# First batch of a pooled-attention and MLP kernel: a broadcast, a bias row and the rests of k placed elsewhere, and the first MLP products in smaller pieces

## The chip, the cores and the metric

The kernel runs on one core of a Trainium2 chip. The metric is device time in microseconds (us) for one execution; the figure given for a kernel is the median of its runs. The core has a matrix engine (TensorE, in the profile PE, with its weight loads as PEld), VectorE (DVE), ScalarE (ACT), GpSimd (POOL) and SyncE (SP), which mostly issues DMA transfers. Each engine works through its own instructions in the order in which the program lists them; between engines semaphores hold the order of data.

## The reference

Eight batches, eight heads, 576 tokens, 64 columns a head; everything in float32.

```python
# attention with k and v averaged over groups of 8 tokens (576 -> 72)
k_p = k.reshape(B, H, 72, 8, D).mean(axis=3)
v_p = v.reshape(B, H, 72, 8, D).mean(axis=3)
scores = matmul(q, k_p.transpose(0, 1, 3, 2)) / sqrt(D)
scores = scores - max(scores, axis=-1, keepdims=True)
attn = exp(scores); attn = attn / (sum(attn, axis=-1, keepdims=True) + 1e-09)
x = matmul(attn, v_p)                      # then laid out as batch x 576 x 512
# mixing over tokens, then an MLP over channels
a1 = alpha1 * x + beta1
tok = einsum('ts,bsd->btd', w_tok, a1)     # w_tok 576 x 576
u = x + lam * tok
a2 = alpha2 * u + beta2
out = u + lam * (maximum(a2 @ w_ch1, 0.0) @ w_ch2)   # 512 -> 2048 -> 512
```

## The kernel before, in words

The 576 tokens of a batch are handled as 512 in four chunks of 128, and a rest of 64; the rests of two batches make one more chunk. So eight batches give 36 chunks, and four chunks make one of nine blocks of 512 tokens for the MLP. While block n goes through the MLP, the attention of batch n+1 is woven into it by a list of pieces with due times (`todo`, L712 to L747). Batch 0 has no MLP to be woven into: its pieces stand one after the other in lines L583 to L662, and this written order is the order of every engine's queue. The change touches only these lines.

The pieces that matter here:

- `keep_warm(n)` (L64): n matmuls of 128x512 on constants, whose result nobody reads.
- `broadcast(i)` (L264): a float32 matmul of a column of ones with one row of `vecs`, which puts that row on all 128 partitions. Row 0 is lam, row 1 lam times alpha1 (multiplied at L262 on DVE). ACT copies the results to `lam_bc` (L586) and `lamal_bc` (L588). `lamal_bc` is first read by `att_X`.
- `cast_q` (L128) and `cast_rem` (L117) turn q and the rests of q and k into bf16; `cast_rem` also sums the rests of k (L123, L124). `sum_k` (L133: L138, L139) and `sum_v` (L412: L416, L418) add the tokens of a group. Ahead of `sum_v(0, 1)` on POOL a memset of one column of the other v tile (L613) makes POOL wait until DVE is done with it.
- `row_of_xs` (L270, instruction L273): the product of beta1 and lam, as an additional row of `xs`, through which beta1 enters the token mixing.
- `att_F` (L362) transposes q for four heads on PE, ACT copies (L373); `att_Frem` (L377) does it for the rests; `att_K` (L393) pools k with matmuls (L401 and, for the rests, L404), copied at L408. `att_S` (L446) makes the scores of one head (L453) and their exponentials on ACT (L455). `att_V`, `att_Vrem` (L421, L437) do for v what `att_K` does for k (matmuls L424, L442; copies L428, L444). `att_AV` (L459) multiplies weights and v (L470, L473) and divides by the row sums on DVE (L475, L477). `att_X` (L480) multiplies x by `lamal_bc` into `xs` (L484, L488).
- `setup_wtok` (L281) transposes a strip of w_tok (PE L288, ACT copy L291), `setup_rowsum` (L294) makes row sums of it (L300, copy L302), `setup_vectors` (L276) turns beta2 (L278, L279), `setup_bias` (L346) makes the MLP's bias from it (L351, L353).
- `mix_T` (L504): five matmuls (L512), the sum u on DVE (L514), and the product with alpha2 (L516). `mix_uT` (L519): four transposes (L527) and an ACT copy into `u_fm` (L529), which holds a block of 512 tokens.
- `mlp_A(n, j, t0, t1)` (L537): four matmuls (L543) for 128 of the 2048 hidden columns and tokens t0 to t1 of the block; the ReLU on ACT (L548) follows when all 512 tokens are there. `mlp_B` (L553, matmuls L566) is the second product.

Loads are issued by SP in the order of the program, except the weights, which POOL issues (`load_wtok` L147, `load_w1` L324, `load_w2` L329). Batch 1's loads (`load_qk(1, 0)` and the following, L631 to L636) stand behind a DVE memset (L82) that comes after `att_AV(0, 5)`. All PSUM results of these pieces but the broadcasts' come from a pool of six buffers (`gp`), the broadcasts' from a pool of two that the MLP's second product uses later.

Of the kernel before, what the change touches and what calls it, by code (L numbers as in the profile page):

```python
# [23 lines left out]
def kernel(  # L24
# [18 lines left out]
    nc = tc.nc  # L43
# [20 lines left out]
    def keep_warm(count):  # L64

        ps = gp("ps_warm")
        for _ in range(count):
            nc.tensor.matmul(out=ps, lhsT=warm[:, 0:P], rhs=warm)
# [48 lines left out]
    def cast_rem(b, eng, copy=None):  # L117
        raw = st1[b]["rem_raw"]
        rq = work.tile([P, 4, D], BF, tag="rem_q", bufs=2, name="rem_q")
        rk = work.tile([P, 2, D], BF, tag="rem_k", bufs=2, name="rem_k")  # L120
        (copy or eng.tensor_copy)(out=rq, in_=raw[:, 0])
        t = raw[:, 1]
        eng.tensor_tensor(out=t[:, 0:2], in0=t[:, 0:2], in1=t[:, 2:4], op=ALU.add)  # L123
        eng.tensor_tensor(out=rk, in0=t[:, 0:1].to_broadcast((P, 2, D)),  # L124
                          in1=t[:, 1:2].to_broadcast((P, 2, D)), op=ALU.add)
        st1[b]["rem"] = rq, rk
# [137 lines left out]
    def broadcast(i):  # L264

        ps = psB.tile([P, DM], FP, tag="ch", bufs=2, name="ps_bc")
        nc.tensor.matmul(out=ps, lhsT=ones_row, rhs=vecs[0:1, i])
        return ps

    def row_of_xs(i, eng):  # L270

        p0 = 64 - 64 * i
        eng.tensor_tensor(out=xs_pool[i][p0:p0 + 1, 4, :], in0=vecs[p0:p0 + 1, 2],  # L273
                          in1=vecs[p0:p0 + 1, 0], op=ALU.mult)

    def setup_vectors():  # L276
        ps = gp("ps_vec")
        nc.tensor.transpose(out=ps[:, 0:4], in_=b2row, identity=identity[0:4, 0:4])  # L278
        nc.scalar.copy(out=b2c_bf, in_=ps[:, 0:4])  # L279

    def setup_wtok(tcx, copy):  # L281

        trc = P if tcx < 4 else REM
        w = wt_bf[0:trc, S * tcx:S * tcx + 640]
        strided = w[:, 0:512].rearrange("p (m c) -> p c m", c=4)
        ps_w = gp("ps_w").bitcast(BF)
        for sc in range(5):
            nc.tensor.transpose(out=ps_w[0:P, trc * sc:trc * sc + trc],  # L288
                                in_=strided[:, sc, :] if sc < 4 else w[:, 512:640],
                                identity=identity_bf[0:trc, 0:trc])  # L290
        copy(out=wtT[:, 0:5, P * tcx:P * tcx + trc],  # L291
             in_=ps_w[:, 0:5 * trc].rearrange("p (s t) -> p s t", t=trc))

    def setup_rowsum(tcx):  # L294

        trc = P if tcx < 4 else REM
        cols = slice(P * tcx, P * tcx + trc)
        ps = gp("ps_rs")
        for sc in range(5):
            nc.tensor.matmul(out=ps[:, 0:trc], lhsT=ones_bf if sc < 4 else ones_lo,  # L300
                             rhs=wtT[:, sc, cols], start=(sc == 0), stop=(sc == 4))
        nc.scalar.copy(out=wtT[64:65, 4, cols], in_=ps[64:65, 0:trc])  # L302
# [43 lines left out]
    def setup_bias(g):  # L346
        ps_bias = gp("ps_bias")
        for i in range(4):
            jc = 4 * g + i
            for cc in range(4):  # L350
                nc.tensor.matmul(out=ps_bias[0:P, i:i + 1], lhsT=w1_of(cc, jc),  # L351
                                 rhs=b2c_bf[:, cc:cc + 1], start=(cc == 0), stop=(cc == 3))
        nc.scalar.copy(out=bias_cols[:, 4 * g:4 * g + 4], in_=ps_bias[0:P, 0:4])  # L353
# [39 lines left out]
    def att_K(b, u, *copies):  # L393

        st = st1[b]
        ps_kp = gp("ps_kp")


        kp = ps_kp[:, 0:320].rearrange("p (r h y) -> p r h y", r=2, h=2)
        for e in range(2):  # L400
            nc.tensor.matmul(out=kp[:, :, :, 8 + 32 * e:40 + 32 * e],  # L401
                             lhsT=st["k"][u][:, e].rearrange("p t d -> p (t d)"), rhs=sel_k)
        kp = ps_kp[:, 0:320].rearrange("p (r y) -> p r y", r=2)
        nc.tensor.matmul(out=kp[:, :, 72:88], lhsT=st["rem"][1].rearrange("p t d -> p (t d)"),  # L404
                         rhs=pool_rem[:, 4 * u:4 * u + 4])
        for j in range(2):
            rows = slice(64 * j, 64 * j + 64)
            copies[j % len(copies)](  # L408
                out=kpT_pool[u][rows, j].rearrange("p r (h x) -> p r h x", h=2)[:, :, :, 0:72],
                in_=kp[rows, :, 8:152].rearrange("p r (h x) -> p r h x", h=2))  # L410
# [26 lines left out]
    def att_Vrem(b, copy):  # L437

        ps_v = gp("ps_v")
        vr = ps_v[:, 0:264].rearrange("p (a x) -> p a x", x=66)  # L440
        for a in range(4):
            nc.tensor.matmul(out=vr[:, a], lhsT=sel_rem[:, a], rhs=vrem_pool[b % 2])  # L442
        for hh, rows in ((0, slice(64, 72)), (1, slice(32, 64))):
            copy(out=vp1_pool[b % 2][hh][rows], in_=vr[rows])  # L444

    def att_S(b, h):  # L446

        st = st1[b]
        u, r, hh = h // 4, h // 2 % 2, h % 2
        ET, n = ET_pool[(8 * b + h) % 6], P if hh else SPG  # L450
        for j in range(2):
            ps_sc = gp("ps_sc")
            nc.tensor.matmul(out=ps_sc[0:n, 0:288], lhsT=kpT_pool[u][:, j, r, 72 * hh:72 * hh + n],  # L453
                             rhs=st["qT"][u][:, h % 4, :])
            nc.scalar.activation(out=ET[0:n, 64 + j:64 + S + j:2], in_=ps_sc[0:n, 0:288],  # L455
                                 func=AF.Exp, bias=0.0, scale=1.0 / 64)
        st["ET"][h] = ET

    def att_AV(b, h):  # L459
        st = st1[b]  # L460
        if "x" not in st:
            st["x"] = work.tile([P, 5, DM], FP, tag="x_tm", bufs=1, name="x_tm")
        hp, hh = h // 2, h % 2
        n = P if hh else SPG
        ET, vp1, x = st["ET"][h][0:n], vp1_pool[b % 2][hh][0:n, hp], st["x"]
        ps_av = gp("ps_av")
        av = ps_av[:, 0:5 * 66].rearrange("p (c x) -> p c x", x=66)
        for c in range(4):
            m0 = 64 + 256 * (c // 2) + c % 2
            nc.tensor.matmul(out=av[:, c, :], lhsT=ET[:, m0:m0 + 256:2], rhs=vp1)  # L470

        r0 = 576 - 64 * (b % 2)
        nc.tensor.matmul(out=av[:, 4, :], lhsT=ET[:, r0:r0 + 128], rhs=vp1)  # L473
        rec = work.tile([P, 5], FP, tag="rec", bufs=2, name="rec")
        nc.vector.reciprocal(out=rec, in_=av[:, :, 64:65])  # L475
        dd = D * h
        nc.vector.tensor_tensor(out=x[:, :, dd:dd + D], in0=av[:, :, 0:64],  # L477
                                in1=rec.unsqueeze(2).to_broadcast((P, 5, D)), op=ALU.mult)

    def att_X(b, h0, h1, eng=nc.vector):  # L480

        x, xs = st1[b]["x"], xs_pool[b % 2]
        cols = slice(D * h0, D * h1)
        eng.tensor_tensor(  # L484
            out=xs[:, 0:4, cols], in0=x[:, 0:4, cols],
            in1=lamal_bc[:, cols].unsqueeze(1).to_broadcast((P, 4, D * (h1 - h0))), op=ALU.mult)
        p0 = 64 * (b % 2)
        eng.tensor_tensor(out=xs[p0:p0 + 64, 4, cols], in0=x[p0:p0 + 64, 4, cols],  # L488
                          in1=lamal_bc[p0:p0 + 64, cols], op=ALU.mult)
# [91 lines left out]


    new_batch(1)  # L583
    keep_warm(4)
    ps_lam = broadcast(0)
    nc.scalar.copy(out=lam_bc, in_=ps_lam)  # L586
    ps_lamal = broadcast(1)
    nc.scalar.copy(out=lamal_bc, in_=ps_lamal)  # L588
    cast_q(0, 0, nc.vector.tensor_copy)
    att_F(0, 0)  # L590
    fill_E()
    sum_k(0, 0, nc.vector)
    cast_rem(0, nc.gpsimd)
    cast_q(0, 1, nc.gpsimd.tensor_copy)
    row_of_xs(0, nc.vector)
    att_Frem(0, (0,), nc.scalar.copy)
    att_K(0, 0, nc.vector.tensor_copy, nc.scalar.copy)
    att_Frem(0, (1,), nc.vector.tensor_copy)
# [7 lines left out]
    att_F(0, 1)  # L606
    att_S(0, 2)
    att_K(0, 1, nc.vector.tensor_copy)
    att_S(0, 3)
    v_00 = st1[0]["v"][0]  # L610
    sum_v(0, 0)
    att_Vrem(0, nc.scalar.copy)
    nc.gpsimd.memset(v_00[:, 0, 0, 0:1], 0.0)  # L613
    sum_v(0, 1, nc.gpsimd)
    att_S(0, 4)
# [19 lines left out]
    load_v(1, 0)  # L635
    load_v(1, 1)  # L636
    att_X(0, 4, 6, nc.gpsimd)
    setup_wtok(2, nc.scalar.copy)
    att_AV(0, 6)
    setup_rowsum(0)  # L640
    setup_rowsum(1)
    setup_wtok(3, nc.scalar.copy)
    att_AV(0, 7)
    att_X(0, 6, 8)
    setup_rowsum(2)
    setup_rowsum(3)
    setup_vectors()
    keep_warm(2)
    mix_T(0, 0)
    mix_T(0, 1)  # L650
    mix_T(0, 2, nc.gpsimd)
    mix_uT((0, 0))
    mix_T(0, 3)
    mix_uT((0, 1))
    setup_bias(0)
    for j in range(4):
        mlp_A(0, j, 0, 256)
        if j in (1, 2):
            mix_uT((0, 1 + j))
    for j in range(4):  # L660
        mlp_A(0, j, 256, 512)
    fill_v(1)  # L662
# [115 lines left out]
```

The softmax here doesn't subtract the row's maximum and nothing guards it: scores larger than these inputs give would overflow.

## Time and profile before

| | |
|---|---|
| median of 5 runs | 369.96 us (369.43 to 370.4) |
| profiled execution | 370.38 us, of which span 368.6 us |
| mean granted clock of PE | 0.995 |
| busy, share of the span: PE, DVE, ACT, POOL | 97%, 60%, 58%, 34% |
| chain that ended last | PE 86%, DMA 4%, POOL 4%, ACT 3% |
| bytes moved by DMA | 43.27 MB, mean 117 GB/s |

The profile is of one execution. Its times are in microseconds from the start of the span. In the timeline a row has start, length, engine, line of the kernel, operation, the tiles written and read, shapes and count; what stands in brackets is how long the engine was idle before it and what ended that. In the chain of waits each row is a piece of the chain that ended last. In the table of stretches the columns are the stretch and its length, then busy time and count for PE, PEld, DVE, ACT and POOL, the granted clock, the busy share of the DMA engines, and GB/s.

### The profile page before, as it was taken

How to read it: one execution, taken by the hardware profiler on the slowest of the kernel's cores; microseconds unless marked ns; L12 is line 12 of the kernel's file. 1: busy time of each engine (PE TensorE's matmuls, PEld its weight loads, DVE VectorE, ACT ScalarE, POOL GpSimd, SP SyncE). 2: the span in 40 equal slices, each digit the busy share in tenths (PEclk: the TensorE clock that was granted, in tenths of full speed). 3: DMA queues.
4: the chain of work that ended last, by engine and by line, in shares of the span. 5: the costliest groups of instructions: out<-in, count | busy, mean ns of one | idle time of the engine just before them, and what ended most of it. 6: DMA issues, size and time to landing. Idle time of an engine off the chain costs nothing.

```text
span 368.6 us, 6142 instructions
## 1 busy us (share of the span) xinstructions
PE 355.8 (97%) x2304; PEld 196.4 (53%) x2346; DVE 219.8 (60%) x437; ACT 213.8 (58%) x420; POOL 126.5 (34%) x182
## 2 busy tenths in 40 slices
PE   7799999999999999999999999999999999999995
PEld 2467555455545554555455555555455545544544
DVE  7774655882786368734876387727863687543011
ACT  3856884389527970698158923895279705712710
POOL 7866923071507241542237140905072410000000
PEclk9989999999999999999999999999999999999999
DMA  7999994039112901192107402570100002002002
GB/s 249 261 227 315 230 283 152 28 123 334 45 46 85 327 27 49 57 307 79 59 28 255 161 30 57 166 250 30 57 29 2 29 31 57 2 28 85 2 29 85
DMA packets 19575, 43.27 MB, mean 117 GB/s; under 512 B 2193, under 2 KB 4565, under 8 KB 19546
## 3 DMA queue, kind: packets, MB, share of 16 engines
q1 hardware_dynamic: 17488, 37.89, 30.5%
q0 software_dynamic: 1888, 4.86, 7.0%
q8 instruction: 18, 0.29, 0.3%
q10 hardware_dynamic: 170, 0.14, 0.2%
q14 instruction: 11, 0.09, 0.1%
HBM read 38.30 MB, written 9.44 MB: 130 GB/s over the span
## 4 chain that ended last, share of the span: by engine, by line
PE 86%; DMA 4%; POOL 4%; ACT 3%; issue 1%; SPq 1%; DVE 0%; POOLq 0%; ACTq 0%
PE ps_ch L566 33%; PE ps_h L543 30%; PE ps_tok L512 11%; DMA rem_raw<-in_q_dram 4%; PE ps_sc L453 4%; PE ps_av L470 2%; PE ps_uT L527 2%; ACT Hj L548 2%; PE ps_q L369 1%; SPq L84 1%; POOL v_u L416 1%; POOL qk_raw L138 1%; PE ps_av L473 0%; ACT qT L373 0%; PE ps_kp L401 0%
## 5 line engine op out<-in xcount | busy, mean ns | idle before, releaser
L543 PE MATMUL ps_h<-u_fm,w 128*128 128x512 bf16 (+1 forms) x575 | 133.7, 373 | 1.4 <-ACT u_fm L529 0.4
L566 PE MATMUL ps_ch<-w,Hj 128*128 128x512 bf16 x489 | 123.9, 379 | 1.3 <-issue 0.2
L548 ACT ACTIVATE Hj<-ps_h,bias_cols 128x512 bf16<-128x512 f32 x144 | 97.1, 691 | 34.5 <-PE ps_h L543 34.0
L543 PEld LDWEIGHTS <-w 128*128 128x128 bf16 x592 | 64.1, 114 | 48.3 <-issue 0.6
L566 PEld LDWEIGHTS <-Hj 128*128 128x128 bf16 x592 | 55.6, 98 | 49.1 <-issue 0.2
L529 ACT COPY u_fm<-ps_uT 128x512 bf16<-128x512 bf16 x36 | 21.0, 587 | 80.7 <-PE ps_uT L527 80.6
L484 POOL TENSOR_TENSOR xs<-x_tm,lamal_bc 128x512 bf16<-128x512 f32 x24 | 30.5, 1271 | 81.1 <-DVE x_tm L477 81.1
L455 ACT ACTIVATE ET<-ps_sc 128x288 f16<-128x288 f32 (+1 forms) x128 | 51.4, 488 | 10.6 <-PE ps_sc L453 10.1
L512 PE MATMUL ps_tok<-xs,wtT 128*128 128x512 bf16 (+1 forms) x200 | 49.3, 379 | 0.3 <-PE ps_vec L278 0.3
L573 DVE TENSOR_TENSOR u_sb<-u_sb,ps_ch 128x512 f32<-128x512 f32 (+1 forms) x37 | 24.9, 672 | 24.9 <-PE ps_ch L566 23.8
L408 DVE CAST kpT<-ps_kp 64x288 bf16<-64x288 f32 x31 | 14.1, 455 | 41.1 <-PE ps_kp L404 40.8
L572 DVE TENSOR_TENSOR ps_ch<-lam_bc,ps_ch 128x512 f32<-128x512 f32 x32 | 22.1, 692 | 24.9 <-PE ps_ch L566 24.8
L514 DVE TENSOR_TENSOR u_sb<-x_tm,ps_tok 128x512 f32<-128x512 f32 (+1 forms) x40 | 27.4, 684 | 11.9 <-PE ps_tok L512 11.8
L477 DVE TENSOR_TENSOR x_tm<-ps_av,rec 128x320 f32<-128x320 f32 x64 | 31.5, 492 | 2.7
L475 DVE RECIPROCAL rec<-ps_av 128x5 f32<-128x5 f32 x64 | 12.3, 192 | 33.7 <-PE ps_av L473 33.4
L512 PEld LDWEIGHTS <-wtT 128*128 128x128 bf16 (+1 forms) x200 | 18.8, 98 | 23.5 <-DVE xs L484 1.9
L138 POOL TENSOR_TENSOR qk_raw<-qk_raw 128x512 f32<-128x512 f32 (+1 forms) x28 | 29.8, 1065 | 1.1
L453 PE MATMUL ps_sc<-qT,kpT 128*128 128x288 bf16 (+1 forms) x128 | 28.6, 299 | 0.7 <-DVE kpT L408 0.5
L516 DVE TENSOR_TENSOR u_bf<-u_sb,al_bc 128x512 bf16<-128x512 f32 (+1 forms) x39 | 27.3, 699 | 1.4
L671 POOL COPY ticks<-ticks 1x1 f32<-1x1 f32 x6 | 1.1, 178 | 73.4 <-DVE ticks L667 73.4
L416 DVE TENSOR_TENSOR v_u<-v_u 128x512 f32<-128x512 f32 (+1 forms) x30 | 24.8, 826 | 0.9 <-DMA v_u<-in_v_dram 0.2
L470 PEld LDWEIGHTS <-ET 72*128 72x128 f16 (+1 forms) x256 | 16.7, 100 | 14.2 <-DVE vp L428 0.5
(115 smaller groups left out, 322.3 us busy)
## 6 DMA issues: line engine op xcount, KB each, us to landing
qk_raw<-in_q_dram SPq DMA_DIRECT2D x16, 512.0 KB, 7.5
qk_raw<-in_k_dram SPq DMA_DIRECT2D x16, 512.0 KB, 6.5
v_u<-in_v_dram SPq DMA_DIRECT2D x32, 256.0 KB, 7.3
out_dram<-u_sb SPq DMA_DIRECT2D x32, 256.0 KB, 2.2
w<-in_moe_w_ch_dram POOLq DMA_DIRECT2D x2, 1024.0 KB, 15.0
w<-in_moe_w_ch_dram POOLq DMA_DIRECT2D x4, 512.0 KB, 10.7
rem_raw<-in_q_dram SPq DMA_DIRECT2D x8, 128.0 KB, 4.6
rem_raw<-in_k_dram SPq DMA_DIRECT2D x8, 128.0 KB, 5.5
```

The source lines that it names most:

```text
L138: eng.tensor_tensor(out=t[:, :, 0:n], in0=t[:, :, 0:n], in1=t[:, :, n:2 * n], op=ALU.add)
L416: eng.tensor_tensor(out=t[:, :, 0:n], in0=t[:, :, 0:n], in1=t[:, :, n:2 * n], op=ALU.add)
L453: nc.tensor.matmul(out=ps_sc[0:n, 0:288], lhsT=kpT_pool[u][:, j, r, 72 * hh:72 * hh + n], rhs=st["qT"][u][:, h % 4, :])
L455: nc.scalar.activation(out=ET[0:n, 64 + j:64 + S + j:2], in_=ps_sc[0:n, 0:288], func=AF.Exp, bias=0.0, scale=1.0 / 64)
L477: nc.vector.tensor_tensor(out=x[:, :, dd:dd + D], in0=av[:, :, 0:64], in1=rec.unsqueeze(2).to_broadcast((P, 5, D)), op=ALU.mult)
L484: eng.tensor_tensor(out=xs[:, 0:4, cols], in0=x[:, 0:4, cols], in1=lamal_bc[:, cols].unsqueeze(1).to_broadcast((P, 4, D * (h1 - h0))), op= ...
L512: nc.tensor.matmul(out=ps_tok, lhsT=wtT[0:kk, at, t0:t0 + P], rhs=xs[0:kk, sc, :], start=(sc == 0), stop=(sc == 4))
L514: nc.vector.tensor_tensor(out=s["u"][p0:p1, :], in0=st1[b]["x"][p0:p1, c, :], in1=ps_tok[p0:p1, 0:DM], op=ALU.add)
L516: eng.tensor_tensor(out=s["u_bf"][p0:p1, :], in0=s["u"][p0:p1, :], in1=al2_bc[p0:p1, :], op=ALU.mult)
L543: nc.tensor.matmul(out=ps_h[:, t0:t1], lhsT=w1_of(cc, j), rhs=u_fm[n][:, cc, t0:t1], start=(cc == 0), stop=(cc == 3))
L548: nc.scalar.activation(out=t, in_=ps_h, func=AF.Relu, bias=bias_cols[:, j:j + 1], scale=1.0)
L566: nc.tensor.matmul(out=ps, lhsT=Hj[n, j][:, 128 * m:128 * m + 128], rhs=w2_of(n, j, cols), start=(j == 0), stop=(j == NJ - 1))
```

## The change

Nothing is computed differently. In the written order of batch 0:

- The four matmuls of `keep_warm(4)` at the very start go.
- `broadcast(1)` moves from the start to behind `att_S(0, 3)`, and its copy to `lamal_bc` behind `att_Vrem`.
- The two sums of the rests of k go from POOL to DVE; the cast of the rests of q stays on POOL.
- `row_of_xs(0)` moves on DVE from ahead of `att_K(0, 0)` to behind `att_K(0, 1)`.
- At the end of the attention `att_AV(0, 6)` and `att_AV(0, 7)` come ahead of one `setup_wtok` and of row sums; `setup_rowsum(3)` and `setup_vectors` move in between the first `mix_T`.
- The first halves of the first four MLP products (256 tokens, 16 matmuls) are done as two quarters (128 tokens each, 32 matmuls), the first quarter for all four before the second; `setup_bias(0)` moves behind them, and the last `mix_uT` behind that.

Lines of the changed kernel are up to two higher than here.

```diff
     new_batch(1)
-    keep_warm(4)
     ps_lam = broadcast(0)
     nc.scalar.copy(out=lam_bc, in_=ps_lam)
-    ps_lamal = broadcast(1)
-    nc.scalar.copy(out=lamal_bc, in_=ps_lamal)
     cast_q(0, 0, nc.vector.tensor_copy)
     att_F(0, 0)
     fill_E()
     sum_k(0, 0, nc.vector)
-    cast_rem(0, nc.gpsimd)
+    cast_rem(0, nc.vector, nc.gpsimd.tensor_copy)
     cast_q(0, 1, nc.gpsimd.tensor_copy)
-    row_of_xs(0, nc.vector)
     att_Frem(0, (0,), nc.scalar.copy)
     att_K(0, 0, nc.vector.tensor_copy, nc.scalar.copy)
     att_Frem(0, (1,), nc.vector.tensor_copy)
...
     att_F(0, 1)
     att_S(0, 2)
     att_K(0, 1, nc.vector.tensor_copy)
+    row_of_xs(0, nc.vector)
     att_S(0, 3)
+    ps_lamal = broadcast(1)
     v_00 = st1[0]["v"][0]
     sum_v(0, 0)
     att_Vrem(0, nc.scalar.copy)
+    nc.scalar.copy(out=lamal_bc, in_=ps_lamal)
     nc.gpsimd.memset(v_00[:, 0, 0, 0:1], 0.0)
     sum_v(0, 1, nc.gpsimd)
     att_S(0, 4)
...
     att_X(0, 4, 6, nc.gpsimd)
+    att_AV(0, 6)
     setup_wtok(2, nc.scalar.copy)
-    att_AV(0, 6)
+    att_AV(0, 7)
     setup_rowsum(0)
     setup_rowsum(1)
     setup_wtok(3, nc.scalar.copy)
-    att_AV(0, 7)
     att_X(0, 6, 8)
     setup_rowsum(2)
-    setup_rowsum(3)
-    setup_vectors()
     keep_warm(2)
     mix_T(0, 0)
+    setup_rowsum(3)
     mix_T(0, 1)
+    setup_vectors()
     mix_T(0, 2, nc.gpsimd)
     mix_uT((0, 0))
     mix_T(0, 3)
     mix_uT((0, 1))
+    for j in range(4):
+        mlp_A(0, j, 0, 128)
+    for j in range(4):
+        mlp_A(0, j, 128, 256)
+        if j == 1:
+            mix_uT((0, 2))
     setup_bias(0)
-    for j in range(4):
-        mlp_A(0, j, 0, 256)
-        if j in (1, 2):
-            mix_uT((0, 1 + j))
+    mix_uT((0, 3))
     for j in range(4):
         mlp_A(0, j, 256, 512)
     fill_v(1)
```

## The prediction

> **What bounds the kernel now.** I read the page first, then the chain that ended last, then each engine's timeline from 0 to 45 us and the granted clock in stretches. TensorE (PE) is busy 97% of the span, and after 33 us nearly without a gap, so only what shifts PE there can move the end. The change lies wholly before 35 us. The chain of waits shows what shifts it (start, length in us, what):
>
> ```profile
> 15.51 0.96 issue
> 16.59 1.27 POOL v_u L416
> ...
> 19.24 0.26 PE ps_v L424
> ...
> 21.96 0.21 DVE rec L475
> ...
> 23.16 10.48 DMA rem_raw<-in_q_dram
> ...
> 37.17 0.73 POOL k_bf L139
> ...
> 37.95 0.29 PE ps_kp L401 x2
> ```
>
> The head hangs on POOL's sum of v (L416), and the "issue" before it is POOL waiting for DVE's own v sum. Then batch 1's loads, issued behind a DVE memset at 21.83, land only at 33.6. POOL sums their k until 37.9, and PE waits for it:
>
> ```profile
> 7.72 1.03 PE L369 MATMUL ps_q<-identity_bf,q_bf 128*128 128x128 bf16 x8
> ...
> 12.15 1.06 PE L369 MATMUL ps_q<-identity_bf,q_bf 128*128 128x128 bf16 x8
> ...
> 14.32 0.40 PE L442 MATMUL ps_v<-vrem,sel_rem 128*128 128x66 f16 x4
> ...
> 16.48 0.23 PE L424 MATMUL ps_v<-v_sum,sel_main 128*128 128x128 f16 x1 [0.83 <-DVE v_sum L418]
> ...
> 24.83 3.41 PE L512 MATMUL ps_tok<-xs,wtT 128*128 128x512 bf16 x15 [0.29 <-PE ps_vec L278]
> ...
> 33.04 1.91 PE L543 MATMUL ps_h<-u_fm,w 128*128 128x256 bf16 x16 [0.24 <-ACT u_fm L529]
> ...
> 35.31 0.61 PE L369 MATMUL ps_q<-identity_bf,q_bf 128*128 128x128 bf16 x8
> ...
> 37.95 0.29 PE L401 MATMUL ps_kp<-sel_k,k_bf 128*128 128x128 bf16 x2 [0.20 <-POOL k_bf L139]
> ```
>
> The last row is a wall: work that PE finishes earlier before it buys only a longer wait there, unless batch 1's k comes earlier too. Between 33.04 and 37.95 PE has 0.2 us of slack and no more; a delay above that reaches the end.
>
> In the head it is DVE and ACT that count:
>
> ```profile
> 9.06 0.82 DVE L273 TENSOR_TENSOR xs<-vecs 1x512 bf16<-1x512 f32 x1
> 10.50 0.45 DVE L408 CAST kpT<-ps_kp 64x288 bf16<-64x288 f32 x1 [0.62 <-PE ps_kp L404]
> ...
> 14.95 1.15 DVE L416 TENSOR_TENSOR v_u<-v_u 128x512 f32<-128x512 f32 x2
> ```
>
> The bias row (L273) costs nothing where it stands: DVE is idle 0.62 us right behind it. At 14.95 DVE goes from K's copies straight into v's sum. ACT is dense from there (eight exponentials):
>
> ```profile
> 16.45 2.96 ACT L455 ACTIVATE ET<-ps_sc 72x288 f16<-72x288 f32 x8
> ```
>
> **The change, part by part.** The profiled execution took 370.38 us, 368.6 of span and 1.78 around it. It is 0.42 above the median, 369.96; shifts are worked out in its trace and set on the median.
>
> *Warm-up matmuls and second broadcast off the front.* The transposes of q (7.72) then need only q_bf, cast on DVE from 5.32 to 5.99: they start near 6.05. But first scores need K(0,0), whose first matmuls stand at 9.08 behind k's sum (L139 ends 9.03). So this part gains nothing at the scores. Removing the four warm-up matmuls should cost nothing: PE was busy from 2.19 to 8.75 and the transposes at 12.15 still took 1.06, against 0.61 at 35.31. [...] The row at 12.15 shows that this busy front did not earn full speed, so I take nothing.
>
> *Rests of k from POOL to DVE.* POOL took 0.62 and 0.78 (L123, L124; rem_k at 10.19). On DVE they follow k's sum at 9.06. Nearest rows: 0.27 and 0.29 for 128x128 (L390, L418) below, POOL's own above. I take 0.65 together: rem_k at 9.7, first scores near 10.5 instead of 11.00. That is the gain of the head, 0.5 us (bounds 0 and 0.6).
>
> *How far that gain goes.* K(0,1) doesn't follow it. DVE's second sum of k starts at 11.29 although DVE was free at 11.14 (back-to-back rows without a wait overlap by some 0.06), so it waited for k's transfer, which doesn't move. Its k_bf is ready at 13.32; K(0,1), on PE at 13.49, can gain only 0.13, and its copies end at 14.8 instead of 14.91.
>
> *Bias row behind K(0,1).* Now it stands ahead of v's sum, with no idle time to hide it: 0.68 (L262, the like product) to 0.82, I take 0.75. Minus 0.1: v's sum runs 15.6 to 17.07 instead of 14.95 to 16.42, +0.65. Queued behind it: PE's ps_v (16.48 to 17.1), AV(0,0) to AV(0,3) (last product on DVE ends 20.05, now 20.65), and POOL's memset L613, with the other v sum and all products of xs on POOL behind that: V(0,1) on PE from 19.24 to 19.9, the last POOL product from 24.14 to 24.8.
>
> *Second broadcast between S(0,3) and Vrem on PE.* One broadcast took 1.8 (from the second's start at 5.9 to the transposes at 7.72, with the array at half speed). S(0,3) ended near 14.3 and, tied to K(0,1), still does. So Vrem goes from 14.32 to 16.1, or to 15.2 if all of it ran at twice the speed. ACT's copies of Vrem (15.67, 0.75) start 0.3 to 0.75 later; the added copy of lamal follows (0.59 each in the two broadcast rows); the eight exponentials start at 17.3 to 17.8 instead of 16.45. ACT is dense, so they end at 20.3 to 20.75 instead of 19.41. V(0,1)'s copies queue behind, then wtT's.
>
> *Reordered end of attention.* AV(0,4) needs V(0,1)'s copy: 20.6 to 21.05 instead of 19.85. Before, AV(0,7) stood behind two row sums and setup_wtok(3), 0.88 us of PE (21.74 to 22.62); now ahead of them. What is late next is DVE: 0.65 a head. Reciprocals for heads 4 to 7: 21.0 to 21.4, then 0.81, 0.7 and 0.65 on. The last product ends at 23.85 to 24.3 (before 23.70), xs is ready 0.98 later, and mix_T(0,0) starts at 24.95 to 25.4 instead of 24.83. I take +0.45, nearer the upper end, since the only rows of a broadcast run at half speed.
>
> *mix_T to the second halves of the MLP.* Before: 8.21 us (24.83 to 33.04). After, in PE pitches from the rows: 20 mix matmuls at 0.216, 4.32; a row sum 0.28 and the vector transpose 0.15, moved in here; four mix_uT at 0.22, 0.88; 32 products of 128 columns at 0.056 (mix_uT's and L300's pitch), 1.79 instead of 16 at 0.109, 1.74; bias 0.53. Sum 7.95. Then the last mix_uT stands behind everything, and the second halves need its copy: tail 0.17, ACT 0.59, two hand-overs, 0.85 uncovered. Total 8.8, +0.59. Before, a product of 256 columns covered most of that copy, and the idle time left was 0.24. The other copies of u_fm are ready in time (the second 6.05 after mix_T starts, needed at 6.09). [...]
>
> *SP's and POOL's queues.* Batch 1's eight loads wait on SP for the memset after AV(0,5), which moves by about 0.5. DMA share is above 1.0 in all stretches from 20 to 36, so what they lose early the weights gain, and landing moves by 0 to 0.5. POOL loses 1.4 us of rests, but its q cast waits for q's transfer, so the weights are issued about 0.5 earlier. Batch 1's k_bf: 37.4 to 38.4.
>
> *Sum.* 0.45 + 0.59 = 1.04 at the second halves; minus the 0.20 of slack at 37.95: +0.84. **Median 370.8**, and a span near 369.4.
>
> **The rivals.** (0.2% is 0.74 us, about what a measurement of this kernel can tell from no change.)
>
> *The clock stays low longer (25%).* In the stretches' rows the granted clock is the third figure from the right:
>
> ```profile
> 18.00:20.00 2.00, 1.73 (x21) 1.34 (x18) 1.90 (x7) 1.85 (x6) 1.92 (x3) 0.61 1.01 185
> 20.00:22.00 2.00, 2.00 (x30) 2.00 (x28) 1.47 (x7) 1.78 (x4) 2.00 (x3) 0.54 1.12 214
> ```
>
> It falls after a thin stretch on PE (16 to 18: 1.14 of 2.00) and returns near 22, after a full one. Now the stretch 18.4 to 21.9 has gaps, for V(0,1) and its copies. If it returns only at 25.3, AV(0,7), three row sums, setup_wtok(3) and the fillers run at half speed (0.53 instead of 0.28 for five matmuls): mix_T starts at 25.6 to 26.2, +0.8 to +1.4, and the sum is +1.2 to +1.8: 371.2 to 371.8.
>
> *Not slower: the wall absorbs it (25%).* The place is 37.95. If the broadcast runs at twice the speed and the bias row hides because v's sum isn't last, the earlier AV(0,7) counts (DVE then ends 0.3 earlier): -0.3 + 0.59 - 0.2 = +0.1, 370.1. If the weights, 0.5 earlier, also bring batch 1's rest forward, the wall itself moves by up to 0.5: 369.4. It decides if mix_T(0,0) starts before 24.5. Against it: ACT is dense, and its 0.59 copy has no hole in that row.
>
> *The head stays the bound as I have it (45%):* +0.4 to +1.1, 370.4 to 371.1. The remaining 5% is for what I don't see.
>
> **How the numbers follow.** Faster than 369.22 needs the whole of the second rival and more: 0.09. Within 0.2% lie the rest of that rival and the lower third of the likeliest case: 0.35. Slower than 370.70: 0.56. Range: from the better part of the second rival, 369.5, to beyond the slow clock, 372.0; about one in ten is left out on each side.
>
> **What would show it.** Right: first scores (L453) near 10.5; the first v sum on DVE at 15.6 behind L273; the row of eight exponentials starting after 17.3; mix_T(0,0) near 25.3; the 256-column products near 34 after a wait of 0.6 or more for u_fm; no wait for k_bf at K(1,0). Wrong: mix_T before 24.8, a wait at the second halves under 0.4, or K(1,0) before 37.9.

## The result, and the profile after

The changed kernel takes 371.07 us (median of 26 runs, 370.02 to 372.08), the kernel before 369.86 beside it (48 runs, 368.74 to 371.05). The ratio is 1.0033, 95% interval 1.0026 to 1.0040: 1.2 us slower, by an interval of 1.0 to 1.5. The profiled execution took 371.52 us with a span of 369.7, against 370.38 and 368.6.

The timeline of PE in the changed kernel, read like that of before (start, length, what, and the idle time ahead of it):

```profile
5.98 1.03 PE L369 MATMUL ps_q<-identity_bf,q_bf 128*128 128x128 bf16 x8 [0.96 <-DVE q_bf L130]
...
10.48 1.36 PE L453 MATMUL ps_sc<-qT,kpT 128*72 128x288 bf16 x4 [0.54 <-DVE kpT L408]
...
14.50 2.07 PE L267 MATMUL ps_bc<-vecs,ones_row 1*128 1x512 f32 x2
16.50 0.40 PE L442 MATMUL ps_v<-vrem,sel_rem 128*128 128x66 f16 x4
...
18.35 0.40 PE L470 MATMUL ps_av<-vp,ET 72*128 72x66 f16 x4 [0.38 <-ACT lamal_bc L611]
...
25.66 1.24 PE L512 MATMUL ps_tok<-xs,wtT 128*128 128x512 bf16 x5 [0.54 <-DVE xs L484]
...
34.57 1.91 PE L543 MATMUL ps_h<-u_fm,w 128*128 128x256 bf16 x16 [0.67 <-ACT u_fm L529]
...
39.13 0.28 PE L401 MATMUL ps_kp<-sel_k,k_bf 128*128 128x128 bf16 x2
```

Two rows of before to set beside these, the first scores and AV(0,0), the first product of weights and v:

```profile
11.00 1.36 PE L453 MATMUL ps_sc<-qT,kpT 128*72 128x288 bf16 x4 [0.54 <-DVE kpT L408]
...
17.09 0.30 PE L470 MATMUL ps_av<-vp,ET 72*128 72x66 f16 x4 [0.38 <-DVE vp L428]
```

The gains at the front are there: q's transposes start 1.74 us earlier and the first scores 0.52 earlier. By AV(0,0) the lead has become a lag of 1.26 (18.35 against 17.09). The second halves of the MLP products come 1.53 late, and the last row, K(1,0), 1.18 late and without a wait. The wall of before, POOL's k_bf, is passed: it is ready 1.3 us ahead of that row, at 37.86:

```profile
37.13 0.73 POOL L139 TENSOR_TENSOR k_bf<-qk_raw 128x256 bf16<-128x256 f32 x1
```

From K(1,0) to the end of the span it is 330.5 to 330.8 us in every profile of this study, so whatever a profiled execution gains or loses, it has gained or lost at K(1,0). The distance of K(1,0) from before's 37.95, set on 370.38, gives the time of all thirteen other profiled executions within 0.13 us.

DVE shows the moves one by one:

```profile
9.07 0.28 DVE L123 TENSOR_TENSOR rem_raw<-rem_raw 128x128 f32<-128x128 f32 x1
9.39 0.29 DVE L124 TENSOR_TENSOR rem_k<-rem_raw 128x128 bf16<-128x128 f32 x1
...
11.55 1.15 DVE L138 TENSOR_TENSOR qk_raw<-qk_raw 128x512 f32<-128x512 f32 x2 [0.92 <-DMA qk_raw<-in_k_dram]
...
15.10 0.68 DVE L273 TENSOR_TENSOR xs<-vecs 1x512 bf16<-1x512 f32 x1
15.81 1.15 DVE L416 TENSOR_TENSOR v_u<-v_u 128x512 f32<-128x512 f32 x2
```

The two rests of k are short on DVE, and 0.92 us of idle time follows soon after: the second sum of k waits for its transfer, as forecast. The bias row (L273) has left idle time for a place straight ahead of v's sum, which starts 0.86 later than before.

The chain that ended last runs through the broadcast now, and POOL is no longer in it:

```profile
14.57 2.00 PE ps_bc L267 x2
16.57 0.35 PE ps_v L442 x4
16.94 0.37 ACT vp L444
17.32 0.37 ACT vp L444
17.72 0.59 ACT lamal_bc L611
18.35 0.40 PE ps_av L470 x4
```

One broadcast takes 2.0 us on PE, holds up Vrem behind it, and its copy takes another 0.59 on ACT ahead of the exponentials, which start at 18.20 instead of 16.45.

**Stages.** All profiles can be laid out alike. The columns are: end of the second sum of k on DVE (L139); from there to AV(0,0); from there to the first mix_T; from there to the second halves of the MLP products; from there to K(1,0). The last two are the sum of the four stages and the ratio to the kernel before with its 95% interval. Each profile is one execution; the ratio is of the medians.

| kernel | k sum ends | to AV | to mix_T | to halves | to K(1,0) | sum | ratio |
|---|---|---|---|---|---|---|---|
| before | 13.32 | 3.77 | 7.74 | 8.21 | 4.91 | 24.63 | 1 |
| after | 13.62 | 4.73 | 7.31 | 8.91 | 4.56 | 25.51 | 1.0033 [1.0026, 1.0040] |
| e1 | 13.19 | 4.99 | 7.31 | 8.91 | 4.56 | 25.77 | 1.0029 [1.0017, 1.0041] |
| e2 | 13.55 | 4.40 | 7.26 | 8.91 | 4.55 | 25.12 | 1.0017 [1.0009, 1.0026] |
| e3 | 13.23 | 4.75 | 7.26 | 8.91 | 4.56 | 25.48 | 1.0030 [1.0017, 1.0043] |
| e4 | 13.26 | 4.87 | 7.30 | 8.69 | 4.55 | 25.41 | 1.0020 [1.0009, 1.0031] |
| e5 | 13.74 | 4.41 | 7.69 | 8.68 | 4.56 | 25.34 | 1.0022 [1.0012, 1.0033] |
| e6 | 13.92 | 3.69 | 8.39 | 8.20 | 4.56 | 24.84 | 1.0004 [0.9993, 1.0016] |
| e7 | 14.65 | 3.69 | 7.26 | 8.37 | 4.61 | 23.93 | 1.0007 [0.9998, 1.0017] |
| e8 | 13.12 | 3.64 | 7.32 | 8.37 | 4.60 | 23.93 | 1.0010 [0.9999, 1.0022] |
| e9 | 13.46 | 3.89 | 7.24 | 8.92 | 4.55 | 24.60 | 1.0015 [1.0003, 1.0027] |
| e10 | 13.04 | 4.59 | 7.33 | 8.20 | 4.56 | 24.68 | 1.0026 [1.0013, 1.0039] |
| e11 | 13.96 | 3.51 | 7.33 | 8.37 | 4.61 | 23.82 | 1.0007 [0.9997, 1.0017] |
| e12 | 13.67 | 3.51 | 7.75 | 7.70 | 4.61 | 23.57 | 0.9973 [0.9961, 0.9984] |

Of the 1.18 at K(1,0), +0.30 lies ahead of the table's stages, +0.96 is the way to AV(0,0), −0.43 the attention's reordered end, +0.70 the MLP's first products and −0.35 the wall. The +0.30 is scatter: after, e4 and e10 have the same order until far behind the second sum of k, and that sum ended at 13.62, 13.26 and 13.04 in their profiles.

A profiled execution can also lie far from its kernel's median. Those of e5, e6 and e7 are each the slowest of their twelve, 0.9 to 1.0 us above the median, and those of e8 and e10 lie 0.7 and 1.0 below it. So stages are compared one by one here, and totals by the ratio.

**The clock of each execution.** The granted clock of PE, averaged over the span, is on record for every execution. It is 0.995 or less where the profile shows a stretch at half clock (before and e8 to e12), and 0.998 or more where it shows none (the others). Of after, 6 executions are of the first kind (median 370.81) and 20 of the second (371.22). Of before, beside e1 to e12, 61 are of the first (369.86) and 50 of the second (370.19). So the second kind is 0.3 to 0.4 us slower and after has more of it, which makes some 0.1 of the 1.2 us. Within either kind after is about 1.0 us slower. That no stretch is recorded doesn't mean full speed throughout, as the last section shows.

### The profile page after: what moved, and what is told of

The parts are those of the page before. It is cut to its first block, busy times and chain, and to the rows that moved or that the text cites. A ratio compares the mean times of both kernels' runs of the same rounds, so it can differ in the third digit from the quotient of the medians.

```text
span 369.7 us, 6167 instructions
## 1 busy us (share of the span) xinstructions
PE 354.8 (96%) x2316; PEld 196.4 (53%) x2358; DVE 219.2 (59%) x439; ACT 213.9 (58%) x420; POOL 124.7 (34%) x180
## 4 chain that ended last, share of the span: by engine, by line
PE 91%; ACT 3%; DMA 2%; DVE 1%; issue 1%; SPq 1%; DVEq 0%
PE ps_ch L566 33%; PE ps_h L543 32%; PE ps_tok L512 12%; PE ps_sc L453 4%; PE ps_av L470 2%; PE ps_uT L527 2%; DMA qk_raw<-in_k_dram 2%; ACT Hj L548 2%; PE ps_q L369 1%; SPq L84 1%; PE ps_av L473 1%; PE ps_kp L401 1%; PE ps_bc L267 1%; ACT qT L373 0%; PE ps_bias L351 0%
## 5 line engine op out<-in xcount | busy, mean ns | idle before, releaser
L543 PE MATMUL ps_h<-u_fm,w 128*128 128x512 bf16 (+2 forms) x591 | 133.5, 368 | 1.7 <-ACT u_fm L529 0.7
L516 DVE TENSOR_TENSOR u_bf<-u_sb,al_bc 128x512 bf16<-128x512 f32 (+1 forms) x39 | 27.8, 712 | 1.4
L470 PEld LDWEIGHTS <-ET 72*128 72x128 f16 (+1 forms) x256 | 17.1, 102 | 14.4 <-DVE vp L428 0.8
L416 DVE TENSOR_TENSOR v_u<-v_u 128x512 f32<-128x512 f32 (+1 forms) x30 | 23.4, 780 | 0.8
```

The source lines that it names most:

```text
L516: eng.tensor_tensor(out=s["u_bf"][p0:p1, :], in0=s["u"][p0:p1, :], in1=al2_bc[p0:p1, :], op=ALU.mult)
L543: nc.tensor.matmul(out=ps_h[:, t0:t1], lhsT=w1_of(cc, j), rhs=u_fm[n][:, cc, t0:t1], start=(cc == 0), stop=(cc == 3))
```

## The experiments

The theory: the broadcast and the bias row in their new places, and the last mix_uT behind the bias, cost more than the head's gain. The rivals: removing the warm-up cost clock, or the new MLP order is the whole of it. Each diff is against the changed kernel unless it says otherwise. Where times in us are given as a loss or gain, they are the ratio's distance from 1 times 370.

### One part undone at a time: e1 to e4

**e1, the warm-up matmuls back.**

```diff
     new_batch(1)
+    keep_warm(4)
     ps_lam = broadcast(0)
```

> The changed kernel with the four warm-up matmuls put back at the very start. My theory (the late second broadcast and the late bias row delay ACT and DVE, and the last mix_uT behind the bias leaves its copy uncovered): no difference to the changed kernel, within 0.15 us, and mix_T(0,0) still near 25.7 us in the profile. Rival, the clock: the front without them leaves the array at half speed until 23.7; then putting them back brings full speed at some point before 22 and gives 0.4 us or more.

1.0029 against 1.0033 for after: no difference that shows. With or without the four matmuls the products of AV (L470) take 0.38 to 0.43 until past 23 us. That is called half speed here: in the trace of before the first three took 0.28 to 0.30 at a granted clock of 1.00, and the next four 0.41 to 0.43 at 0.50. So putting the warm-up back doesn't bring that fast stretch back, and e8 below has it without the warm-up (0.28 to 0.30 until 18.5).

**e2, the second broadcast back at the front**, with its copy to `lamal_bc`.

```diff
     nc.scalar.copy(out=lam_bc, in_=ps_lam)
+    ps_lamal = broadcast(1)
+    nc.scalar.copy(out=lamal_bc, in_=ps_lamal)
...
-    ps_lamal = broadcast(1)
...
-    nc.scalar.copy(out=lamal_bc, in_=ps_lamal)
```

> The changed kernel with the second broadcast and its copy back at their old place behind the first. My theory: PE has the room there (it idles 1.0 and 1.5 us before 8.5), first scores stay at 10.5; S(0,4)'s exponentials start 2 us earlier, AV(0,4) about 0.55 earlier (then behind POOL's sum of v), so mix_T(0,0) near 25.1 and -0.55 us at the end (-0.3 to -0.7). Rival, the bias row: DVE's late sum of v sets AV(0,0) and V(0,1) by itself, and the broadcast only hides behind it: 0 to -0.15 us.

1.0017: of the 1.2 us lost, 0.6 is back, the most of the four, though e4's 0.5 is within the noise of it. But AV(0,0) is still 0.63 later behind k's sum than before (4.40 against 3.77). PE's timeline of e2 says why:

```profile
17.29 0.29 PE L424 MATMUL ps_v<-v_sum,sel_main 128*128 128x128 f16 x1 [1.29 <-DVE v_sum L418]
17.95 0.40 PE L470 MATMUL ps_av<-vp,ET 72*128 72x66 f16 x4 [0.38 <-DVE vp L428]
```

With the broadcast gone PE waits 1.29 us for v's sum on DVE, the one behind the bias row.

**e3, the bias row ahead of the second sum of k**, into DVE's idle time there.

```diff
     att_S(0, 1)
+    row_of_xs(0, nc.vector)
     sum_k(0, 1, nc.vector)
...
-    row_of_xs(0, nc.vector)
     att_S(0, 3)
```

> The changed kernel with the bias row on DVE ahead of the second sum of k, where DVE idles 0.9 us for k's transfer. My theory: AV(0,0) waits for the copy of lamal and V(0,1) for PE's order, so this alone gives nothing: 0 to -0.15 us, though the sum of v ends 0.7 earlier. Rival, the bias row sets the head: -0.5 us or more, AV(0,0) before 18.

1.0030, and 4.75 to AV(0,0): nothing gained, though v's sum ended at 16.20 instead of 17.29. Together, e2 and e3 show two delays that lie side by side. The broadcast's way (PE, ACT) costs 0.96 and the bias row's way (DVE) 0.63 on the stage to AV(0,0); the longer one counts, and taking it away uncovers the other. The kernels below that have neither (e6, e7, e8 and e11) need 3.5 to 3.7 on this stage, before 3.77.

**e4, the MLP bias behind the last mix_uT** instead of ahead of it.

```diff
-    setup_bias(0)
     mix_uT((0, 3))
+    setup_bias(0)
```

> The changed kernel with setup_bias(0) and the last mix_uT exchanged, so that the bias matmuls cover the copy of u_fm. My theory: the wait of 0.67 us at the second halves of the MLP products shrinks to under 0.2, the second halves start 0.5 earlier (34.05), and the end comes 0.5 us earlier (-0.35 to -0.6), since K(1,0) no longer waits for POOL. Rival, the wall: what PE gains here turns into a wait at K(1,0) (0.5 us there for k_bf), and the end stays within 0.15.

1.0020, which is 0.5 us back by the medians, with an interval of some 0.4 either way. The wait for u_fm falls from 0.67 to 0.17, as it should, yet the stage only from 8.91 to 8.69. The bias had covered something: the transposes now wait for DVE. PE, DVE and POOL of e4:

```profile
33.05 0.40 PE L527 MATMUL ps_uT<-identity_bf,u_bf 128*128 128x128 bf16 x4
...
34.12 1.91 PE L543 MATMUL ps_h<-u_fm,w 128*128 128x256 bf16 x16 [0.17 <-ACT u_fm L529]
```

```profile
31.44 1.55 DVE L516 TENSOR_TENSOR u_bf<-u_sb,al_bc 128x512 bf16<-128x512 f32 x1
```

```profile
31.41 1.03 POOL L130 CAST q_bf<-qk_raw 128x1024 bf16<-128x1024 f32 x1
```

The product with alpha2 (L516) takes 1.55 us here, against a mean of 0.71 over all 39 on the page, and for its first 1.0 us POOL casts batch 1's q. In after it is just as long, but there the bias, 0.50 on PE, lies beside its end.

### Parts together, and the head alone: e5 to e8

**e5, e2 and e4 together.**

```diff
+    ps_lamal = broadcast(1)      # both as in e2
+    nc.scalar.copy(out=lamal_bc, in_=ps_lamal)
...
-    setup_bias(0)
     mix_uT((0, 3))
+    setup_bias(0)
```

> The changed kernel with both repairs together: the second broadcast back at its old place, and the last mix_uT ahead of setup_bias(0). Each alone gave back about 0.5 us. My theory: they lie one after the other on the same path (mix_T(0,0) starts earlier; from there to the second halves is shorter), so they add up: -1.0 us to the changed kernel (-0.8 to -1.2), which is the kernel before within 0.25. Rival, they hide behind the same wait (the wall at K(1,0), or POOL's products of xs): together not more than -0.6.

1.0022: no better than either alone, a miss. The stages carry both gains (4.41 and 8.68), but the stage to mix_T is 0.43 longer than in e2 (7.69 against 7.26). The wait for xs isn't what differs, for it is 0.98 here and 1.17 in e2. POOL's sum of v started 0.40 late for its transfer, and the products of AV were at half speed (0.40 to 0.43) until past 23 us, in e2 only until 21.3 (0.28 from then on). That is one execution, the slowest of its twelve, so why the gains didn't add up is not shown.

```profile
18.00 2.06 POOL L416 TENSOR_TENSOR v_u<-v_u 128x512 f32<-128x512 f32 x2 [0.40 <-DMA v_u<-in_v_dram]
```

**e6, the kernel before with only the rests of k on DVE** and the bias row in the idle time of e3.

```diff
-    cast_rem(0, nc.gpsimd)
+    cast_rem(0, nc.vector, nc.gpsimd.tensor_copy)
     cast_q(0, 1, nc.gpsimd.tensor_copy)
-    row_of_xs(0, nc.vector)
...
+    row_of_xs(0, nc.vector)
     sum_k(0, 1, nc.vector)
```

> The kernel before with only this: the rests of k summed on DVE, and the bias row on DVE in its idle time ahead of the second sum of k. My theory: first scores may come up to 0.5 earlier, but K(0,1) waits for k's transfer and the second sum, and the end does not move: 0 within 0.2 us to the kernel before. Rival, first scores set the head: -0.4 us or more.

1.0004, within the interval no change. The first scores come 0.41 earlier in the profile (10.59), and that is worth nothing that shows: DVE waits 0.45 us for k's transfer ahead of the second sum, and everything behind keeps to that. Nor do the rests and the row, put there, do harm that shows.

**e7, every cost hidden**: the second broadcast behind the first transposes of q, the row as in e3, the bias as in e4, and the second halves in quarters too.

```diff
     att_F(0, 0)
+    ps_lamal = broadcast(1)      # with its copy; the later ones go
...
     mix_uT((0, 3))
+    setup_bias(0)                # moved; the row as in e3
     for j in range(4):
-        mlp_A(0, j, 256, 512)
+        mlp_A(0, j, 256, 384)
+    for j in range(4):
+        mlp_A(0, j, 384, 512)
```

> The changed kernel with each moved step where the profile shows idle time: second broadcast behind the first transposes of q (PE idle 1.5 us there), bias row ahead of the second sum of k, last mix_uT ahead of setup_bias(0), and the second halves of the first four MLP products in quarters too, so that the first of them need only the third copy of u_fm. My theory: sum of v ends at 16.2, mix_T(0,0) starts near 24.2, the second halves near 32.2 without a wait, and PE then reaches K(1,0) at about 36.8, where it waits 0.1 to 1.0 us for POOL's k_bf, which depends on batch 1's transfers: -0.5 to -1.0 us to the kernel before, less than mix_T's gain. Rival, no wall: no wait at K(1,0), and all of mix_T's and the second halves' gain arrives, -1.2 us or more.

1.0007: nearly the whole loss is gone, but the gain that was expected beyond before isn't there. The stages behind k's sum are 0.70 shorter than before's. In the profile, the slowest of twelve executions, that is spent ahead of them: the second sum of k ends at 14.65. Some of it is scatter, since already the first sum of k ended at 9.73, in after at 9.16. DVE and POOL of e7:

```profile
12.09 1.97 DVE L138 TENSOR_TENSOR qk_raw<-qk_raw 128x512 f32<-128x512 f32 x2
```

```profile
12.58 1.78 POOL L434 TENSOR_TENSOR rem_v_raw<-rem_v_raw 64x256 f32<-64x256 f32 x2
```

The pair of sums that opens the second sum starts only behind the bias row, and takes 1.97 instead of 1.15 while POOL sums the rests of v.

**e8, e7 with batch 1's loads ahead of AV(0,3)** on SP, with the memset that they wait for.

```diff
     att_AV(0, 2)
+    load_qk(1, 0, nc.vector)     # and the five loads behind it
     att_S(0, 7)
```

> The kernel of the preceding run, with batch 1's loads and their memset on DVE three heads earlier (ahead of AV(0,3) and not behind AV(0,5)). My theory: DMA is full anyway, but these loads then share earlier with the second half of w1, which has time until 40 us; k_bf of batch 1 comes 0.5 to 1.5 earlier, the wait at K(1,0) goes, and another 0.2 to 0.8 us arrive at the end. Rival, total bytes set the landing: k_bf comes at the same time, no difference within 0.15; or w1 comes late and costs time at the products of the second 1024 columns.

1.0010, the same as e7. Batch 1's k_bf is ready at 36.08 and PE needs it at 37.05, without a wait; in e7 it was 37.24 and 38.58. So the wall no longer binds, and moving it further pays nothing that shows. The profiled executions of e7 and e8 lie at opposite ends of their runs (371.14 and 369.51), and their four stages sum to 23.93 in both: nearly all of the 1.6 us between them is the end of k's second sum, 14.65 and 13.12.

### Head and tail apart, and two attempts at a better one: e9 to e12

**e9, the kernel before with only the last part of the change** (row sum and vectors in between, quarters, bias, last mix_uT).

```diff
+    for j in range(4):
+        mlp_A(0, j, 0, 128)
+    for j in range(4):
+        mlp_A(0, j, 128, 256)
+        if j == 1:
+            mix_uT((0, 2))
     setup_bias(0)
-    for j in range(4):           # the halves of before
...
+    mix_uT((0, 3))
```

> The kernel before with only the last part of the change: one row sum and the vector transpose in between the first mix_T, quarters, and setup_bias(0) ahead of the last mix_uT. My theory: from mix_T(0,0) to the second halves it takes 8.9 us instead of 8.2, with a wait of 0.67 there, while mix_T(0,0) itself hardly comes earlier: +0.3 to +0.6 us to the kernel before. Rival, the late broadcast is the whole loss: 0 within 0.15.

1.0015, slower by 0.55 us (0.1 to 1.0), as expected. The second halves wait 0.67 for u_fm, as they do in after.

**e10, the changed kernel with that part undone.** The diff is that of e9, backwards.

> The changed kernel with the last part of the change undone (everything from the third row sum on as before), so with the moves in the head and AV(0,6), AV(0,7) in their new place alone. My theory: mix_T(0,0) as late as in the changed kernel (25.2 to 25.7), 8.2 us from there to the second halves: -0.4 to -0.6 us to the changed kernel, still +0.5 to +0.8 to the kernel before. Rival, the tail is the whole loss: equal to the kernel before within 0.2.

1.0026: only 0.26 of 1.2 us comes back, less than the 0.4 to 0.6 expected, though the intervals overlap. The stage is 8.20 again, as before. The head alone costs 0.96 (0.5 to 1.4), the tail alone 0.55, both 1.22: the tail seems to count for less once the head is late, though the intervals allow a plain sum. This profile happens to show the cheap end of the broadcast:

```profile
14.12 1.12 PE L267 MATMUL ps_bc<-vecs,ones_row 1*128 1x512 f32 x2
...
17.03 0.23 PE L424 MATMUL ps_v<-v_sum,sel_main 128*128 128x128 f16 x1 [1.07 <-DVE v_sum L418]
```

At 1.12 instead of 2.07 the broadcast is no longer what holds AV(0,0); v's sum, behind the bias row, is, with a wait of 1.07. The stage still takes 4.59. The profile is not a typical one: it is of the first kind of clock, whose 5 executions have a median of 370.02, and the other 7 one of 371.08.

**e11, e8 with the broadcast back at the front and five matmuls of 128x512 whose result nobody reads**, between 8 and 14 us.

```diff
     att_F(0, 0)
+    keep_warm(2)
...
     att_Frem(0, (0,), nc.scalar.copy)
+    keep_warm(1)                 # and one each after att_Frem(0, (1,)) and att_S(0, 2)
```

> The kernel with earlier loads, with the second broadcast right behind the first and five additional matmuls of 128x512 on constants, which nobody reads, where PE idles between 8 and 14 us. The clock's share: in the profiles so far PE runs at half speed until 21.5 to 23.9, except in two, where it was released near 15 for one stretch of 3.4 us. If gaps in PE's work hold it back, these fillers bring full speed by 12 to 13 (the second set of eight transposes takes 0.6 and not 1.06), mix_T(0,0) comes 0.5 us or more earlier after the second sum of k, and the end 0.3 to 1.0 us earlier than without them, below the kernel before. Rival, the head hangs on DVE and ACT and not on PE's speed: transposes faster, the end unchanged within 0.2; or the fillers themselves delay the scores: +0.2 or more.

1.0007, as e7 and e8. The fillers do what they are for: the transposes of q near 12 us take 0.61 instead of 1.06. They don't move the end. Its 12 runs lie within 369.96 to 370.32, where those of before beside them spread over 2.7 us. All twelve are of the first kind of clock (0.993 to 0.995).

**e12, against the kernel before**: the rests on POOL, the row and both broadcasts as before; no `keep_warm(4)`, the five fillers, the loads as in e8, AV(0,6) and AV(0,7) as in after, both halves in quarters, the last mix_uT ahead of the bias.

```diff
-    keep_warm(4)                 # the fillers as in e11, the loads as in e8
...
+    att_AV(0, 6)
     setup_wtok(2, nc.scalar.copy)
-    att_AV(0, 6)
+    att_AV(0, 7)
...
+    mix_uT((0, 3))
     setup_bias(0)                # quarters before and after, as in e7
```

> The head of the kernel before (rests of k on POOL, bias row and second broadcast at their old place), with the fillers of the preceding run instead of the warm-up matmuls, batch 1's loads three heads earlier, AV(0,6) and AV(0,7) ahead of the row sums, quarters with the last mix_uT ahead of setup_bias(0), and the third row sum and the vector transpose ahead of mix_T. In the preceding profile DVE's sums of the rests took 1.0 and its second sum of k 1.56 while POOL ran, and PE waited 1.4 us for xs ahead of mix_T. My theory: these collisions ate the gain there; without DVE's part in them k's second sum ends near 13.3, mix_T(0,0) starts near 24.3, the second halves 8.0 to 8.3 later, and the runs lie as close together as with the fillers: -0.3 to -0.8 us to the kernel before. Rival, the collisions are beside the path and k's transfer alone sets the head: equal to the preceding kernel, 0 to +0.4.

0.9973, interval 0.9961 to 0.9984: faster than before, 369.56 against 370.38 beside it, and by the ratios faster than after. (Before's median beside the other kernels was 369.7 to 370.0, so the gain may be smaller than the 1.0 us of the ratio; within the first kind of clock alone it is 0.6, 369.73 of 7 against 370.31 of 8.) The stages sum to 23.57. The 7.70 from mix_T to the second halves is the shortest of all kernels, but a row sum and the vector transpose stand ahead of mix_T here, so the stage before it is longer. From AV(0,0) to the second halves it is 15.45, in e7, e8 and e11 15.6 to 15.7. PE reaches K(1,0) at 37.24, with k_bf ready at 36.51:

```profile
12.16 0.61 PE L369 MATMUL ps_q<-identity_bf,q_bf 128*128 128x128 bf16 x8
...
32.63 1.96 PE L543 MATMUL ps_h<-u_fm,w 128*128 128x128 bf16 x32
...
37.24 0.28 PE L401 MATMUL ps_kp<-sel_k,k_bf 128*128 128x128 bf16 x2
```

Keeping DVE clear of POOL, the reason expected, is not shown: the first two adds of k's second sum took 1.56 here as well, that sum ended at 13.67, and mix_T started at 24.93 rather than 24.3. Which of its parts pays was not separated.

## Why the prediction was right

Forecast 370.8 and slower as the likeliest; measured 371.07. Point by point:

- **Front.** Transposes near 6.05: 5.98. Rests of k on DVE 0.65: 0.57. First scores near 10.5: 10.48. No gain beyond them, since k's transfer holds the second sum: its wait is 0.92, and e6 shows the head's gain alone to be worth nothing that can be measured. The gain itself comes and goes: in e4 and e10, with the same order up to there, first scores stood at 10.94 and 10.84, because one sum of the rests took four times as long on DVE (last section). The forecast had bounds of 0 to 0.6 for it.
- **Warm-up.** Taken at nothing: e1 bears that out, as far as its interval of 0.6 to 1.5 us against before can tell.
- **Bias row.** 0.75 taken, 0.68 measured, v's sum at 15.81 (forecast 15.6). It is on the path only where the broadcast isn't longer (e2, e10).
- **Broadcast.** The upper end was right: 2.0 on PE. The exponentials start later than forecast, at 18.20 instead of 17.3 to 17.8: the broadcast began at 14.50 rather than 14.3 and took 0.2 more, so Vrem started at 16.50 instead of 16.1 and the rest follows. In e10 it took 1.12, so the lower end occurs too.
- **First mix_T.** This is the term that was mis-sized: +0.45 forecast, +0.83 measured. 0.30 of it is the end of k's sum, which scatters from run to run; from there on it is +0.53 (0.96 − 0.43).
- **mix_T to the second halves.** +0.59 forecast, +0.70 measured, with the wait of 0.67 for the last copy that was named; e9 and e10 move it from 8.2 to 8.9 and back. The price of 128-column products by the trace (56 ns) held: 24 of them take 1.34 in the chain.
- **Loads.** The memset ahead of batch 1's loads came 1.58 later (23.41 against 21.83), not the 0.5 forecast, since AV(0,5) did. Of the weights w_tok was issued 0.55 earlier, as forecast, but w_ch1 0.30 later. Neither mattered: k_bf was ready at 37.86, inside the 37.4 to 38.4 forecast and 0.03 from before.
- **The wall.** It is gone, as forecast. It gave back 0.35 rather than 0.20: where nothing waits, the row of K(1,0) starts 0.16 before the row ahead of it ends, so the wait shown in the profile understates the room by that much.
- **Sum.** +0.84 forecast, +1.18 at K(1,0) in the trace, +1.2 between the medians. Against the forecast, mix_T is 0.38 and the products 0.11 worse, the wall 0.15 better. The mechanism held; the size is short by 0.37 us.

The first rival was half right. PE does run at half speed until past 23 us (0.38 to 0.43 for the products of AV), as it supposed, and mix_T at 25.66 even lies at the start of the 25.6 to 26.2 that it named, but 0.30 of that is the late end of k's sum. Where it put the price, hardly anything shows. From AV(0,0) to mix_T it is 7.31 in after and 7.26 in e3, where the products are back at 0.28 by 21.6: with AV(0,7) early, DVE sets most of this stage (mix_T waits for its xs, 0.54 in after and 1.17 in e3). The kinds of clock above leave it some 0.1 of the 1.2 us. The order of before seems to pay for it: e6, slow until 22.14 at least (0.43 for that product), takes 8.39 there against 7.74, in one execution. The second rival fell: mix_T started at 25.66, far from its 24.5.

Open are three things. e7, e8 and e11 save 0.7 to 0.8 us behind k's sum, and their medians show none of it; e7 and e11 spend it ahead of that (14.65, 13.96), but their other executions weren't profiled. The late v and the slow products of e5 were seen in one execution only. And e12's parts weren't told apart.

## What to carry to other kernels

Before moving work off one wait, look at what the next stage is tied to: here an earlier start of 0.5 us met a transfer that didn't move, and the moved work (a broadcast of 2.0 us, a copy of 0.59) landed on a stretch without idle time. When two delays lie side by side, undoing either one can show little (e3) or only the difference to the other (e2); undo both. And split a gain or loss into stages between fixed events, since the start of the chain alone scatters by half a microsecond.

## What the runs showed of the hardware

**A DVE sum took longer where POOL's cast had started first.** POOL and DVE in the timeline of e4:

```profile
8.50 1.16 POOL L130 CAST q_bf<-qk_raw 128x1024 bf16<-128x1024 f32 x1 [0.48 <-DMA qk_raw<-in_q_dram]
8.68 1.12 DVE L123 TENSOR_TENSOR rem_raw<-rem_raw 128x128 f32<-128x128 f32 x1
```

A sum that takes 0.28 alone took 1.12 and ended 0.14 after POOL's cast (9.80 and 9.66); in e5 it was the same one, with 1.12, and in e1, e10 and e11 the next one, L124, with 1.00, 1.15 and 1.01 against 0.29. In these five profiles POOL's cast was the first to start, by 0.02 to 0.29 us; in the other six with the rests on DVE both sums had started before it, and took 0.28 and 0.29. In the five the two rests took 1.3 to 1.4 us rather than the 0.6 of after, and the first scores came at 10.84 to 10.98, against 11.00 before. What makes the sum wait is not shown.

**The recorded stretch at half clock had one length.** In before the granted clock fell to one half from about 18.44 to 21.84 us (0.50 in every piece of half a microsecond or less from 18.5 to 21.8; 0.61 and 0.54 in the two stretches of 2 us: 1.56 and 1.84 us at half). By the same working it was 3.40 us in e8, e9, e11 and e12 and 3.44 in e10, from different starts. The column has a gap, though: in after it reads 1.00 from 8 to 26 us, while the lengths of the AV products (0.38 to 0.43, where before's took 0.28 to 0.30 at 1.00 and 0.41 to 0.43 at 0.50) say half speed up to 23.5. Lengths of like rows are the safer reading.

**Batch 1's data came no later, though they were asked for later.** Batch 1's first load was issued at 23.51 instead of 21.93, yet POOL's first cast of its data began at 33.50, before at 33.69. The DMA share was above 1.0 from 20 to 34 us in both (1.02 to 1.14 in stretches of 2 us). In e8, issued 4.2 us ahead of e7 (19.15 against 23.36), k_bf was ready only 1.2 us earlier.
